# A new order for the beginning of a Fourier mixer with a low-rank channel product

## The chip, the cores and the metric

The kernel runs on one core of a Trainium2 chip. The metric is the device time of one execution in microseconds (us); lower is better. The engines are TensorE (PE, with its weight loads shown as PEld), VectorE (DVE), ScalarE (ACT), GpSimd (POOL) and the DMA queues, which SyncE (SP) and POOL issue to. Each engine works off its own list of instructions in order; semaphores hold an instruction until what it needs is there.

## The reference

```python
X = np.fft.fft(x, axis=1)              # x: 8 batches, 3136 rows, 256 channels, f32
X = np.fft.fft(X, axis=2).real         # the mixed rows
h = X.transpose(0, 2, 1) @ U @ V       # U: 3136 x 32, V: 32 x 3136, along the rows
u = X + h.transpose(0, 2, 1)
out = u + np.maximum(u @ w_ch1, 0) @ w_ch2     # 256 -> 1024 -> 256
```

## The kernel before

**Fourier transform.** The transform of a batch is two products with cosines and sines: along the 3136 rows (`seq`) and along the 256 channels (`chan`). Symmetry makes the first small. `x` is loaded as forward rows `xf` (gathers that POOL issues, one of each quarter q) and as rows read in reverse `xr` (plain DMAs from SP). VectorE folds them: `along_d` adds or subtracts channel d and 256-d (lines L350 and L352, even or odd quarters, `EV` and `OD`), into `EOF_` and `EOR_`; `alone` copies the two channels that have no partner (L356, POOL); `mirror` (L360, L363) combines forward and reverse; `half` (L368) gives `GO` (odd output rows) and `GE`, and `fourth` (L372) gives `GC` (even output rows). `seq(b, par, typ, pn)` then multiplies the folded rows with tables: `par` 1 for odd and 0 for even outputs, `typ` 0 for the sine channels and 1 for the cosine ones, and `pn` 0 and 1 for two products whose sum and difference are two mirrored halves of the output. The first product is copied out of PSUM by ScalarE (`ev`, L432); the second is joined with it by VectorE (L452 the sum into one half, L454 or L456 the difference into the other) into the rows `A` and `B`. `chan` (L473, L475) multiplies `A` and `B` with the channel tables `MC` and `MSN`, in four parts of 392 columns, and ScalarE copies the result to `S` and `T`. For sine, odd outputs, one row of `B` is negated by POOL (L465).

**Tables.** The cosine and sine tables (`TABE`, `TABO`, `TABS`) are made on the chip at the start: POOL's iota, two VectorE instructions per phase, ScalarE's sine; ScalarE copies mirrored parts, VectorE halves the entries that would count twice (`halve`, L310 and L312) and multiplies others with alternating signs (`other_even`, L344, `other_odd`, L335, with the row `srow` of -1 and 1).

**U.** The low-rank factor U goes through the same transform: `fold_u` folds it on VectorE (L209 to L223), `transform_u(t)` gives three steps: two of small matmuls (L256) and the copy of their result into spare columns of the tables. Every `seq` then yields the product with the transformed U in 32 more columns; the joins write it to `tab` (L459, L462). `lowrank` (L485, L488) turns `tab` into `TA`, and writes one row of `VA` (L489), in which V lies.

**Main loop.** The rows of all batches are taken in 49 chunks of 512. `front(c)` adds the low-rank part (L511) to `S` and `T` on VectorE (`u`, L519); `first_product` (L531) and a ReLU on ScalarE (L533) give `h`, and `second_product` (L547), added to the transposed `u` on VectorE (L553 to L556), gives the output. The fold, `seq` and `chan` of the next batches are spread between, as steps with a due number (eight per chunk).

**What sets the order.** Up to the main loop the order of each engine's instructions is that of the code (`manual_schedule`). In the main loop a planner orders them by its own reckoning of when each can start, so VectorE may do folds of a later batch ahead of a sum that stands earlier in the code. Tiles wait for their last readers; `xf`, `xr`, `EOF_`, `EOR_` and `GE` exist once, `GO`, `GC`, `VA` and `TA` twice. PSUM has three buffers of the name `dft`, three `p1` and two `p2`.

The first batch before the change: all of the U work comes ahead of the folds; the folds first make channels 0 to 127 and 256 (sine), then 128 to 255 (cosine); and then each `seq` is followed by its joins, all eight `chan`, `lowrank`, and `front(0)`.

Of the kernel before, what the change touches and what calls it, by code (L numbers as in the profile page):

```python
# [16 lines left out]
P = 128  # L17
PQ = 98
KP = PQ + 1
NI = 4  # L20
# [11 lines left out]
def kernel(  # L32
# [82 lines left out]
    nc.gpsimd.iota(xidx[:], pattern=[[S // 4, B], [S // 16, 4]], base=97, channel_multiplier=-1)  # L115
    load_0(moe_U, UF, UR, 0, R)
    load_r(moe_U, UR, 0, 0, 4, R)
    for q in range(4):
        load_f(moe_U, UF, 0, q, R)
    load_0(x, xf, xr, 0, D)  # L120
    for q0 in (1, 0):
        load_r(x, xr, 0, q0, 2, D)
    iota(kev[:, 0:NT], [[-2, 2], [-4, NT // 2]], 392)
    iota(kev[:, NT:2 * NT], [[-2, NT]], 391)
    for q in (0, 2, 1, 3):
        load_f(x, xf, 0, q, D)
# [23 lines left out]
    zeros(nc.vector, 0)  # L150

# [13 lines left out]
    srow = cpool.tile([KP, 2 * NT], BF16, name="srow")  # L165
# [31 lines left out]
    phe = gen.tile([KP, 2, 2 * NT], I32, name="phe", bufs=1)  # L197
    uy = cpool.tile([KP, 2, 2, 2, NI * R], FP32, name="uy")
# [7 lines left out]
    def fold_u():  # L206
# [12 lines left out]
        for c in range(2):  # L219
            nc.vector.tensor_tensor(GUC[c].rearrange("p t i r -> p t (i r)"), ueven[:, :, 0],  # L220
                                    ueven[:, :, 1], op=AL.add if c == 0 else AL.subtract)
            nc.vector.tensor_single_scalar(NUC[c][:], GUC[c][:, :, 2, :], -1.0, op=AL.mult)
            nc.vector.tensor_single_scalar(NUO[:, :, c, :], GUO[:, :, c, 2 - 2 * c, :], -1.0, op=AL.mult)  # L223
# [27 lines left out]
    def transform_u(t):  # L251
# [22 lines left out]
        def even_k():  # L274
            pu = PU[t] = psum.tile([P, 16, R], FP32, tag="dft", name="pu", bufs=3)
            for c, i in enumerate((3, 1)):
                for io in range(NI):
                    dst = pu[:kp(io), 2 * io + c, :]
                    if io % 2 == 0:
                        group(dst, [(wo(t, i, io, nm), go(i, nm)) for nm in range(2)])  # L280
                    else:
                        group(dst, [(we(t, i, io), gc(i, io))])
# [25 lines left out]
    def halve(t):  # L308
        for lo, hi in ((0, TE - NT), (T2, WE)):
            nc.vector.tensor_single_scalar(TABE[t][:, 3, lo:hi], TABE[t][:, 3, lo:hi], hv[:KP], op=AL.mult)  # L310
        v = TABS[t][:, 0, 1, off_t(t, 3):off_t(t, 3) + NT]
        nc.vector.tensor_single_scalar(v, v, hv[:KP], op=AL.mult)  # L312
# [12 lines left out]
    def cosine_odd(i):  # L325

        sgn = 1.0 if i == 0 else -1.0
        nc.scalar.activation(both(1, i, 1, 0, 1, NT), both(0, i, NT - 1, NT - 1, -1, NT),
                             AF.Copy, scale=sgn)
        nc.scalar.activation(TABO[1][:, 0, i // 2, 0:2 * NT], TABO[0][:, 0, i // 2, 2 * NT - 1::-1][:, 0:2 * NT],  # L330
                             AF.Copy, scale=sgn)

    def other_odd(t):

        nc.vector.tensor_tensor(TABO[t][:, 1, :, 0:2 * NT], TABO[1 - t][:, 0, :, 0:2 * NT],  # L335
                                strip(srow[:], 0, [[0, 2], [1, 2 * NT]]), op=AL.mult)

    def other_even(t):

        def cells(u, nm):  # L340
            v = TABS[u][:, nm, 0, :]
            return bass.AP(v.tensor, v.offset + off_t(u, 1),
                           [v.ap[0], [WS + off_t(u, 3) - off_t(u, 1), 2], [1, NT]])
        nc.vector.tensor_tensor(cells(t, 1), cells(1 - t, 0),  # L344
                                strip(srow[:], 0, [[0, 2], [1, NT]]), op=AL.mult)
# [8 lines left out]
    def alone(qs, src, dst):  # L354

        nc.gpsimd.tensor_copy(dst[:, qs, :, 128:257:128], src[:, qs, :, 0:129:128])  # L356
# [36 lines left out]
    def seq(b, par, typ, pn):  # L393
# [8 lines left out]
        d = ST[b]  # L402
        pt = psum.tile([P, QW], FP32, tag="dft", name="pt", bufs=3)
        mm = []

        def add(t, col, odd):

            if par == 0:
                for c in range(2):
                    g = GC[b % 2][0 if (c == 0) == (t == 1) else 1]  # L410
                    lo, hi, at = ((0, TE - NT + NE, 0), (TE - NT + NE, WE, TE - NT))[c]
                    for i in ((0, 2) if odd else (1, 3)):
                        mm.append((at, g[:kp(i), i, col:col + P], TABE[t][:kp(i), i, lo:hi]))
            else:
                for i in ((0, 2) if odd else (1, 3)):
                    at = 0 if odd else NT * slot(t, i)
                    tab = TABO[t] if odd else TABS[t]
                    for nm in range(2):
                        mm.append((at, GO[b % 2][:kp(i), nm, i, col:col + P],
                                   tab[:kp(i), nm, i // 2, :]))  # L420
        if typ == 1:
            add(1, 128, pn == 1)
        else:
            add(0, 0, pn == 1)
            add(1, 256, (pn == 1) == (par == 1))
        for n, (at, w, rhs) in enumerate(mm):
            nc.tensor.matmul(pt[:, at:at + rhs.shape[-1]], w, rhs, start=(n == 0),  # L427
                             stop=(n == len(mm) - 1), skip_group_check=True)
        if pn == 0:
            ev = d["ev"] = wp.tile([P, QW], FP32, tag="ev", name="ev", bufs=2)  # L430
            w = WO if par else QW
            nc.scalar.copy(ev[:, :w], pt[:, :w])  # L432
            if par == 1:
                eh = d["eh"] = wp.tile([P, 2 * NT], FP32, tag="eh", name="eh", bufs=2)
                nc.vector.tensor_tensor(eh[:, 0:NT], ev[:, NT - 1::-1], ev[:, WO - 1:WS - 1:-1],
                                        op=AL.subtract)
                nc.vector.tensor_tensor(eh[:, NT:2 * NT], ev[:, 0:NT], ev[:, WS:WO], op=AL.add)
            return
        ev = d["ev"]
        dst = d["A"] if typ == 1 else d["B"]  # L440
        if par == 0:
            def src(v):
                return strip(v[:], 1, [[WS, 2], [1, NT]])
# [3 lines left out]
            u0 = TE - NT  # L447
        else:
            p_, e_ = pt[:, 0:2 * NT], d["eh"][:]
            up, dn = dst[:, 783::-2], dst[:, 785:HALF:2]  # L450
            u0 = None
        nc.vector.tensor_tensor(up, p_, e_, op=AL.add)  # L452
# [4 lines left out]
        if par == 0:  # L457
            nc.vector.tensor_tensor(dst[:, 784:785], pt[:, 0:1], ev[:, 0:1], op=AL.add)
            nc.vector.tensor_tensor(d["tab"][:, typ, par, :], pt[:, TE - NT:TE - NT + NE],  # L459
                                    ev[:, TE - NT:TE - NT + NE], op=AL.add)  # L460
        else:
            nc.vector.tensor_tensor(d["tab"][:, typ, par, :], pt[:, 2 * NT:WO],  # L462
                                    ev[:, NT:WS], op=AL.add)
            if typ == 0:
                nc.gpsimd.tensor_single_scalar(dst[0:1, 785:HALF:2], dst[0:1, 785:HALF:2], -1.0,  # L465
                                               op=AL.mult)

    def chan(b, ch, h):
# [3 lines left out]
        pt = psum.tile([P, TE], FP32, tag="dft", name="pst", bufs=3)  # L472
# [6 lines left out]
    def lowrank(b):  # L479
        d = ST[b]  # L480
        pt = psum.tile([R, 256], FP32, tag="dft", name="ptt", bufs=3)
        n = 0
        for typ in range(2):
            for par in range(2):
                nc.tensor.matmul(pt[:], d["tab"][:, typ, par, :], MDT[typ][:],  # L485
                                 start=(n == 0), stop=(n == 3))
                n += 1
        nc.scalar.copy(TA[b % 2][:R, :], pt[:])  # L488
        nc.vector.tensor_tensor(VA[b % 2][R:R + 1, HALF + 1:S], d["S"][0:1, HALF - 1:0:-1],  # L489
# [76 lines left out]
    def transform(b):  # L566

        yield from fold(b)
        for par, typ in ([(1, 0), (0, 0), (1, 1), (0, 1)] if b == 0 else
                         [(0, 1), (0, 0), (1, 1), (1, 0)]):  # L570
            for pn in range(2):
                yield lambda par=par, typ=typ, pn=pn: seq(b, par, typ, pn)
# [3 lines left out]
        yield lambda: lowrank(b)  # L576
# [7 lines left out]
    nc.vector.memset(srow[:, 0:2 * NT:2], -1.0)  # L584
    nc.vector.memset(srow[:, 1:2 * NT:2], 1.0)
# [35 lines left out]
    for t in range(2):  # L621
        halve(t)
    other_even(0)
    other_even(1)
    us, uc = transform_u(0), transform_u(1)
    fold_u()
    other_odd(0)
    other_odd(1)
    us[0]()
    us[1]()  # L630
    uc[0]()
    uc[1]()
    us[2]()
    uc[2]()
    along_d(OD, xr, EOR_, 0)
    alone(OD, xr, EOR_)
    zeros(nc.gpsimd, 1)
    for s in range(2):
        nc.gpsimd.memset(VA[s][:].bitcast(I32), 0)
        nc.gpsimd.memset(TA[s][:], 0.0)  # L640
        nc.gpsimd.memset(TA[s][R:R + 1, 0:1], 1.0)
        nc.gpsimd.memset(TA[s][R:R + 1, P:P + 1], -1.0)
    nc.gpsimd.iota(pint[:], pattern=[[0, 1]], base=D, channel_multiplier=-1)
    nc.gpsimd.memset(pint[0:1], P)
    along_d(EV, xr, EOR_, 0)
    alone(EV, xr, EOR_)
    along_d(EV, xf, EOF_, 0)
    alone(EV, xf, EOF_)
    mirror(0, slice(0, 128), AL.subtract)
    mirror(0, slice(256, 258), AL.add)  # L650
# [3 lines left out]
    phase(pd[:], lrow.rearrange("p a l -> p (a l)"), pcol[:], 17)  # L654
    sine(MSN[:, 0:128], pd[:, 0:128], 17, -1)
# [4 lines left out]
    along_d(OD, xf, EOF_, 0)  # L660
    alone(OD, xf, EOF_)
    mirror(1, slice(0, 128), AL.subtract)
    mirror(1, slice(256, 258), AL.add)
# [87 lines left out]
```

## Time and profile before

| what | value |
|---|---|
| median of 3 runs | 490.22 us (490.13 to 490.26) |
| the profiled execution, its time | 490.67 us |
| the profiled execution, its span | 488.9 us |
| busy: PE, DVE, ACT, POOL | 449.7, 342.7, 273.3, 88.1 us |
| main loop, L531 and L547 together | 2352 matmuls, 413.8 us busy |
| granted TensorE clock, mean | 0.99 |

The span is what the profile's times count from. Busy times of matmuls overlap in TensorE's pipeline, so 449.7 us does not mean that many microseconds at its peak. In the lines shown below, a row of a timeline has the start, the busy time, the engine, the line of the code, the operation, what it writes and reads with the shape, and in brackets how long the engine was idle before and what ended it. A row of the chain of waits has the start, the time that the chain spends there, and the engine and line; L12 is line 12 of the kernel.

### The profile page before, as it was taken

What the parts mean: (1) busy time and instruction counts of PE and PEld (TensorE: products, weight loads), DVE (VectorE), ACT (ScalarE), POOL (GpSimd) and SP (SyncE); (2) the same over time, 40 slices, a digit from 0 to 9 for tenths busy, and PEclk for the clock granted to TensorE, in tenths of its full rate; (3) what the DMA queues carried; (4) which work ended last, traced back from release to release, by engine and by line L of the source; (5) the groups of instructions that cost most, each with busy time, mean ns of one, the idle gap of its engine ahead of it and who ended that gap; (6) DMA issues with size and microseconds to landing.
All of it is one profiled execution on the core that took longest, in us unless ns stands there. A gap on an engine that the chain in (4) does not pass through costs nothing.

```text
span 488.9 us, 8177 instructions
## 1 busy us (share of the span) xinstructions
PE 449.7 (92%) x3096; PEld 299.9 (61%) x3096; DVE 342.7 (70%) x771; ACT 273.3 (56%) x533; POOL 88.1 (18%) x109
## 2 busy tenths in 40 slices
PE   0364799999999999999999999999999999999997
PEld 0342267666766666666766676666766676666665
DVE  5999699999999999997984358343743374434333
ACT  5331655665557554765566655756466556656562
POOL 7745230424144321610010001000010001000000
PEclk9997899999999999999999999999999999999999
DMA  5778389499839995595232422334223352333433
GB/s 149 157 135 236 64 152 254 134 253 260 231 89 220 245 249 163 134 272 142 70 104 65 131 67 68 102 89 129 67 66 86 108 88 86 88 98 99 128 90 126
DMA packets 87275, 67.14 MB, mean 137 GB/s; under 512 B 53920, under 2 KB 80556, under 8 KB 87236
## 3 DMA queue, kind: packets, MB, share of 16 engines
q1 hardware_dynamic: 81588, 51.86, 41.2%
q0 software_dynamic: 5648, 14.76, 11.8%
q8 instruction: 24, 0.39, 0.3%
q14 instruction: 15, 0.12, 0.1%
HBM read 29.26 MB, written 25.69 MB: 112 GB/s over the span
## 4 chain that ended last, share of the span: by engine, by line
PE 79%; DVE 16%; issue 2%; POOL 1%; ACT 1%; DVEq 0%; POOLq 0%
PE p L547 32%; PE p L531 31%; PE pt L427 6%; PE ph L511 4%; PE pst L473 3%; PE pst L475 2%; DVE eof L352 1%; DVE B L452 1%; DVE eof L350 1%; DVE u L519 1%; DVE eor L350 1%; DVE eor L352 1%; DVE A L452 1%; DVE B L456 1%; POOL uf L56 1%
## 5 line engine op out<-in xcount | busy, mean ns | idle before, releaser
L533 ACT ACTIVATE h<-p 128x512 bf16<-128x512 f32 x392 | 218.5, 597 | 139.6 <-PE p L531 139.4
L531 PE MATMUL p<-u,w 128*128 128x512 bf16 x784 | 210.1, 379 | 2.7 <-DVE u L519 2.7
L547 PE MATMUL p<-w,h 128*128 128x256 bf16 x1568 | 203.7, 273 | 0.0
L547 PEld LDWEIGHTS <-h 128*128 128x128 bf16 x1568 | 153.1, 98 | 59.2 <-DVE o L556 0.3
L531 PEld LDWEIGHTS <-w 128*128 128x128 bf16 x784 | 75.5, 98 | 59.8 <-issue 3.8
L553 DVE TENSOR_TENSOR o<-p,ut 128x4 f32<-128x4 f32 (+1 forms) x100 | 16.1, 161 | 111.3 <-PE p L547 111.2
L56 POOL DMA_INDIRECT xf<-in_x_dram,xidx x32 | 40.2, 1257 | 72.8 <-DVE eof L352 51.4
L465 POOL TENSOR_SCALAR B<-B 1x392 bf16<-1x392 bf16 x8 | 14.6, 1823 | 181.9 <-DVE tab L462 129.7
L556 DVE TENSOR_TENSOR o<-p,ut 128x254 f32<-128x254 f32 (+1 forms) x100 | 40.5, 405 | 0.0
L555 DVE TENSOR_TENSOR o<-p,ut 128x254 f32<-128x254 f32 (+1 forms) x100 | 40.5, 405 | 0.0
L519 DVE TENSOR_TENSOR u<-ph,S 128x512 bf16<-128x512 f32 (+15 forms) x64 | 34.9, 554 | 0.1
L432 ACT COPY ev<-pt 128x424 f32<-128x424 f32 (+1 forms) x32 | 16.4, 513 | 32.9 <-PE pt L427 21.4
L519 DVE TENSOR_TENSOR u<-ph,T 128x512 bf16<-128x512 f32 (+15 forms) x64 | 34.8, 553 | 0.0
L427 PEld LDWEIGHTS <-go 98*128 98x128 bf16 x192 | 19.4, 102 | 18.9 <-DVE go L368 7.1
L511 PE MATMUL ph<-va,ta 128*128 128x512 bf16 (+18 forms) x128 | 29.7, 329 | 0.5 <-ACT ta L488 0.5
L427 PE MATMUL pt<-te,gc 98*128 98x229 bf16 (+1 forms) x192 | 24.8, 268 | 0.3 <-DVE tab L459 0.2
L473 PE MATMUL pst<-A,mc 128*128 128x392 bf16 (+1 forms) x64 | 22.7, 355 | 2.3 <-DVE A L452 1.4
L427 PE MATMUL pt<-to,go 98*128 98x424 bf16 x96 | 21.8, 367 | 2.6 <-DVE tab L462 2.6
L475 PE MATMUL pst<-B,msn 128*128 128x392 bf16 (+1 forms) x64 | 22.7, 354 | 0.0
L427 PEld LDWEIGHTS <-gc 98*128 98x128 bf16 x192 | 18.6, 100 | 6.4 <-DVE tab L459 2.8
L477 ACT CAST S<-pst 128x392 bf16<-128x392 f32 (+1 forms) x32 | 15.7, 489 | 12.1 <-PE pst L475 12.1
L256 PE MATMUL pu<-guo,ts 99*98 99x32 bf16 (+1 forms) x16 | 2.3, 239 | 19.3 <-DVE guo L213 19.3
(120 smaller groups left out, 364.1 us busy)
## 6 DMA issues: line engine op xcount, KB each, us to landing
out_dram<-o SPq DMA_DIRECT2D x48, 512.0 KB
xr<-in_x_dram SPq DMA_DIRECT2D x7, 1568.0 KB
xr<-in_x_dram SPq DMA_DIRECT2D x2, 784.0 KB
ut<-u SPq DMA_TRANSPOSE x49
xf<-in_x_dram,xidx POOLq DMA_INDIRECT x32, 6.6
w<-in_moe_w_ch_dram POOLq DMA_DIRECT2D x1, 512.0 KB, 7.8
out_dram<-o SPq DMA_DIRECT2D x4, 128.0 KB
va<-in_moe_V_dram POOLq DMA_DIRECT2D x2, 196.0 KB, 5.2
```

The lines of the kernel that those rows point to most:

```text
L56: nc.gpsimd.indirect_dma_start(out_, None, bass.AP(t.tensor, t.offset, [[w, rows], [1, w]]), bass.IndirectOffsetOnAxis(idx, 0), element_of ...
L427: nc.tensor.matmul(pt[:, at:at + rhs.shape[-1]], w, rhs, start=(n == 0), stop=(n == len(mm) - 1), skip_group_check=True)
L432: nc.scalar.copy(ev[:, :w], pt[:, :w])
L473: nc.tensor.matmul(pt[:, :hi - lo], MC[:, h * P:(h + 1) * P], d["A"][:, lo:hi], start=True, stop=False)
L475: nc.tensor.matmul(pt[:, :hi - lo], MSN[:, h * P:(h + 1) * P], d["B"][:, lo:hi], start=False, stop=True)
L511: nc.tensor.matmul(ph[:, col:col + hi - lo], TA[b % 2][:, s * P:(s + 1) * P], VA[b % 2][:, lo:hi], start=True, stop=True)
L519: nc.vector.tensor_tensor(u[:, s, col:col + hi - lo], ph[:, col:col + hi - lo], src, op=AL.add)
L531: nc.tensor.matmul(p1[:], W1[:, s, j * P:(j + 1) * P], k["u"][:, s, :], start=(s == 0), stop=(s == 1))
L533: nc.scalar.activation(k["h"][:, j, :], p1[:], AF.Relu)
L547: nc.tensor.matmul(p2[:, t % w, :], h[:, j, rs], W2[:, j, :], start=(j == 0), stop=(j == JT - 1))
L555: nc.vector.tensor_tensor(o[:, ts, 1:P], p2[:, :w, 1:P], ut[:, ts, 1:P], op=AL.add)
L556: nc.vector.tensor_tensor(o[:, ts, P + 1:D], p2[:, :w, P + 1:D], ut[:, tT, P - 1:0:-1], op=AL.add)
```

## The change

Only the beginning changes, and the first batch. In words:

- **Loads.** On SP, U's reverse rows are loaded first and x's odd reverse quarters come ahead of x's single rows. On POOL the iota `kev` stands after two of U's four gathers instead of after all four.
- **Tables.** `halve` goes from VectorE to POOL. `other_even` becomes four strided POOL instructions, `other_odd` four strided ScalarE copies; `srow` is gone. The zero columns of `GO` and `GC` of the first buffer are set by POOL.
- **Folds.** VectorE's order is: odd reverse rows, `fold_u`, even reverse rows, channel tables, forward rows. The negations of the folded U and the first batch's `alone` are ScalarE's.
- **U in the first batch.** The products of batch 0 leave out the 32 columns for U (`ne` is 0); `u_alone` computes them by 48 matmuls of its own. `transform_u(1)` stands between the products, its result in `p2`.
- **Joins.** The joins of batch 0 are split: first the outputs up to 784 (`high=False`) of all four groups, then `u_alone`, `lowrank` and the first `chan`, then the mirrored outputs (`low=False`), each followed by one `chan`. `EB` is 4, so four `ev` are kept.
- **Into the main loop.** Four `chan` steps (columns from 785) and the one-row `VA` (`mirror_row`) get the due numbers 0, 1, 4, 5 and 6.
- **The rest.** `VA` is zeroed by two memsets over partitions 32 to 63 and 64 to 127 instead of one over all. POOL's DMAs of W1, V and W2 follow the table work; the small `gate` read ahead of the second batch's loads is gone.

The diff, cut to its core:

```diff
+    load_r(moe_U, UR, 0, 0, 4, R)
     load_0(moe_U, UF, UR, 0, R)
-    load_r(moe_U, UR, 0, 0, 4, R)
-    for q in range(4):
+    load_r(x, xr, 0, 1, 2, D)
+    load_0(x, xf, xr, 0, D)
+    load_r(x, xr, 0, 0, 2, D)
+    for q in range(2):
         load_f(moe_U, UF, 0, q, R)
...
     iota(kev[:, NT:2 * NT], [[-2, NT]], 391)
+    for q in range(2, 4):
+        load_f(moe_U, UF, 0, q, R)
...
     def halve(t):
         for lo, hi in ((0, TE - NT), (T2, WE)):
-            nc.vector.tensor_single_scalar(TABE[t][:, 3, lo:hi], TABE[t][:, 3, lo:hi], hv[:KP], op=AL.mult)
+            nc.gpsimd.tensor_single_scalar(TABE[t][:, 3, lo:hi], TABE[t][:, 3, lo:hi], hv[:KP], op=AL.mult)
...
     def other_odd(t):
+        for n, sgn in enumerate((-1.0, 1.0)):
+            nc.scalar.activation(TABO[t][:, 1, :, n:2 * NT:2], TABO[1 - t][:, 0, :, n:2 * NT:2],
+                                 AF.Copy, scale=sgn)
     def other_even(t):
...
+        for n, sgn in enumerate((-1.0, 1.0)):
+            nc.gpsimd.tensor_single_scalar(cells(t, 1, n), cells(1 - t, 0, n), sgn, op=AL.mult)
...
+    def u_alone(b, tag):
+        d = state(b)
+        pt = psum.tile([P, 2, R], FP32, tag=tag, name="ptu", bufs=BUFS[tag])
+        for typ in range(2):
+            mm = []
+            for t, col in ((1, P),) if typ else ((0, 0), (1, 256)):
+                for c in range(2):
+                    g = GC[b % 2][0 if (c == 0) == (t == 1) else 1]
+                    lo = TE - NT + NE * c
+                    mm += [(g[:kp(i), i, col:col + P], TABE[t][:kp(i), i, lo:lo + NE]) for i in range(NI)]
+                for i in range(NI):
+                    tab, lo = (TABS[t], off_u(t, i)) if i % 2 else (TABO[t], 2 * NT)
+                    mm += [(GO[b % 2][:kp(i), nm, i, col:col + P], tab[:kp(i), nm, i // 2, lo:lo + NE])
+                           for nm in range(2)]
+            for n, (w, rhs) in enumerate(mm):
+                nc.tensor.matmul(pt[:, typ, :], w, rhs, start=(n == 0), stop=(n == len(mm) - 1))
+        nc.scalar.copy(d["tab"][:, :, 0, :], pt[:])
...
     for t in range(2):
+        other_odd(t)
+    for t in range(2):
         halve(t)
+    for t in range(2):
+        other_even(t)
+    zeros(nc.gpsimd, 0)
+    for part in range(2):
+        along_d(OD, xr, EOR_, part)
     fold_u()
+    negatives()
+    for part in range(2):
+        along_d(EV, xr, EOR_, part)
...
     phase(pd[:], lrow.rearrange("p a l -> p (a l)"), pcol[:], 17)
+    alone(OD, xr, EOR_, nc.scalar.copy)
+    alone(EV, xr, EOR_, nc.scalar.copy)
+    alone(EV, xf, EOF_, nc.scalar.copy)
+    alone(OD, xf, EOF_, nc.scalar.copy)
...
+    us[0]()
+    us[1]()
+    us[2]()
     nc.gpsimd.dma_start(out=W1[:, 0, :], in_=moe_w_ch1[0:P, :])
     gather(w1t[:], moe_w_ch1, D, pint[:], H, 0)
     for s in range(2):
+        nc.gpsimd.memset(VA[s][R:2 * R].bitcast(I32), 0)
+        nc.gpsimd.memset(VA[s][2 * R:P].bitcast(I32), 0)
...
+    zeros(nc.gpsimd, 1)
+    for part in range(2):
+        along_d(EV, xf, EOF_, part)
+    mirror(0, slice(0, 128), AL.subtract)
+    mirror(0, slice(128, 258), AL.add)
+    along_d(OD, xf, EOF_, 0)
+    mirror(1, slice(0, 128), AL.subtract)
+    mirror(1, slice(256, 258), AL.add)
+    for cols in (slice(0, 128), slice(256, 258)):
+        half(0, 1, cols)
+    seq(0, 1, 0, 0, "dft", False)
+    seq(0, 1, 0, 1, "p1")
+    sin_odd = dict(ST[0])
+    for cols in (slice(0, 128), slice(256, 258)):
+        half(0, 0, cols)
+        for c in range(2):
+            fourth(0, c, cols)
+    uc[0]()
+    uc[1]()
+    uc[2]()
+    seq(0, 0, 0, 0, "dft")
+    seq(0, 0, 0, 1, "p1")
+    sin_even = dict(ST[0])
+    along_d(OD, xf, EOF_, 1)
+    mirror(1, slice(128, 256), AL.add)
+    half(0, 1, slice(128, 256))
+    seq(0, 1, 1, 0, "dft", False)
+    seq(0, 1, 1, 1, "p1")
+    cos_odd = dict(ST[0])
+    half(0, 0, slice(128, 256))
+    for c in range(2):
+        fourth(0, c, slice(128, 256))
+    seq(0, 0, 1, 0, "dft")
+    seq(0, 0, 1, 1, "p2")
+    cos_even = dict(ST[0])
+    groups = ((1, 0, sin_odd), (0, 0, sin_even), (1, 1, cos_odd), (0, 1, cos_even))
+    for par, typ, kept in groups:
+        apart(0, par, kept)
+        join(0, par, typ, kept, high=False)
+    u_alone(0, "p2")
+    lowrank(0)
+    chan(0, 0, 0, "dft")
+    for par, typ, kept in groups[:3]:
+        join(0, par, typ, kept, low=False)
+        chan(*((0, 0, 1, "p1"), (0, 1, 0, "p1"), (0, 1, 1, "p1"))[groups.index((par, typ, kept))])
+    join(0, 0, 1, cos_even, low=False)
     load_x(1)
...
-    due = {}
+    due = {0: [lambda: chan(0, 2, 0)], 1: [lambda: chan(0, 2, 1)], 4: [lambda: chan(0, 3, 0)],
+           5: [lambda: chan(0, 3, 1)], 6: [lambda: mirror_row(0)]}
```

## The prediction

> **What bounds the kernel now.** I read the page first, then the beginning in the chain of waits, the timeline of POOL and PE there, and busy time by stretch. The stretches (PE, PEld, DVE, ACT, POOL, granted clock, DMA):
>
> ```profile
> 54.00:62.00 8.00, 5.68 (x26) 2.26 (x25) 7.97 (x11) 4.59 (x9) 2.13 (x2) 1.00 0.39 86
> 62.00:70.00 8.00, 7.61 (x55) 5.06 (x53) 8.00 (x13) 3.88 (x8) 4.16 (x3) 1.00 0.65 129
> 90.00:110.00 20.00, 20.00 (x139) 13.09 (x137) 19.92 (x37) 13.60 (x28) 5.22 (x4) 1.00 0.71 196
> 200.00:300.00 100.00, 100.00 (x703) 67.87 (x702) 72.36 (x161) 60.40 (x116) 7.43 (x9) 1.00 0.45 122
> ```
>
> From 62 us on TensorE is full; the loop costs what it costs, so the change is worth the time by which the loop starts earlier, less what it adds or stalls there. The loop starts with the second L531 at 55.42. What stands ahead of it is, in the chain:
>
> ```profile
> 12.40 3.85 DVE te L310 x2
> ...
> 28.70 1.80 DVE eos L363 x2
> 30.51 0.73 DVE go L368 x2
> ...
> 40.10 0.76 DVE gc L372 x2
> ...
> 47.20 0.49 PE pst L473
> ...
> 53.08 0.93 DVE va L489
> ```
>
> VectorE carries it to 47.2 (folds, then joins), then 16 matmuls of `chan` (to 52.6, about 0.33 each), the one-row `va` (0.93), and the sums `u`. Two DVE steps are too long: two halvings of 0.30 each took 3.85, the 0.69 mirror 1.72. POOL shows why:
>
> ```profile
> 13.50 0.54 POOL L146 MEMSET go<- 99x504 int32 x1
> 14.46 1.42 POOL L639 MEMSET va<- 128x1568 int32 x1
> 28.85 1.03 POOL L689 CAST w<-w1t 128x1024 bf16<-128x1024 f32 x1
> 144.07 3.55 POOL L465 TENSOR_SCALAR B<-B 1x392 bf16<-1x392 bf16 x1
> ```
>
> The halving stood still until POOL's unbroken run of memsets ended at 16.13; the mirror grew by 1.03, the length of the CAST. At 144.07 the reverse: a 1.30 us POOL step takes 3.55 while two DVE folds (1.20, 1.21, no longer than elsewhere) run.
>
> TensorE in the first batch:
>
> ```profile
> 31.21 1.70 PE L427 MATMUL pt<-ts,go 98*128 98x228 bf16 x8 [4.37 <-DVE go L368]
> 32.70 2.86 PE L427 MATMUL pt<-to,go 98*128 98x424 bf16 x8
> 35.40 1.75 PE L427 MATMUL pt<-te,gc 98*128 98x229 bf16 x16
> ```
>
> The first 16 run at half pace (0.35 for 424 columns), the next at 0.109 each. I call the first of these starts T0: 31.2 now. T0 to loop start is 24.2.
>
> **What the change does to T0.** DVE drops 0.97 us of zero memsets and 0.44 of `srow`; `kev` comes after two U gathers instead of four (2 x 1.27 earlier). ACT's table work (8.75 to 15.65, 6.9 long) then starts near 6.2 and ends at 13.1; the four alternating-sign copies it takes over (rows like L330, 0.42 apart) end at 14.8. It is not last. The x rows issued first on SP let DVE do both odd reverse folds (2 x 1.13) before U is there, so they are free. The U fold waits for its last gather: in before issued at 6.28, landed 7.9 later; now pushed back 0.6 by `kev`: 14.8. Behind that, to T0, DVE has: U fold 3.5 (17.09 to 21.18 less four negations, now ACT), even reverse 2.27, phase of the channel tables 0.9, even forward 2.27, mirrors 1.4, odd forward half 1.13, mirror 0.78, odd half 0.75: 13.0. T0 would be 27.8. x lands at 18.7 to 21.8 in the trace (gathers issued at 8.05 to 11.99, 9.8 to 11.0 to land; their issue times stay), before each fold needs it. `us` on TensorE (about 3.2, as `uc`) needs the strips: with POOL done by 24 it ends at 27.2, before T0; each microsecond that POOL is later than 28 would move T0. The four `alone` pairs go to ACT (0.25 each on POOL), idle there; without that cover they would cost 1.0.
>
> Against it: POOL takes over six halvings and four sign strips, each 196 columns, from 13.7 on (after gathers to 12.94 and small iotas). No row has 99x196 on POOL. The 1x392 TENSOR_SCALAR gives 0.65 each by halves; the 1024-column CAST at 1.03 against the 16-column one at 0.25 gives 0.39. So 3.9 to 6.5 us, of which 2.8 to 5.4 lie after 14.8, where DVE wants two SBUF inputs. By the CAST row the one waits for the other, and POOL holds first. I take 4.1, the middle, since the operation is L465's but the layout of six is the CAST's. T0 = 31.9, no earlier than now. If POOL waits instead, DVE loses nothing (27.8).
>
> The Trainium skill, page "SBUF — State Buffer", section "Who interferes with whom", says that a DVE instruction with two SBUF inputs contends with a GpSimd instruction that reads SBUF, not with one that only writes. The trace agrees on both: 1.72 beside the CAST, but L209 its usual 0.42 beside the second VA memset (16.38 to 17.79). By that rule alone the whole 2.8 to 5.4 stands and the zero memsets moved to POOL are free; the page "GPSIMD Engine Reference", section "Engine selection", calls one-input work there roughly line-rate, by which the lower end would hold and the time be 1.3 us less than my sum.
>
> **From T0 to the loop.** Now TensorE is the longer chain, because DVE's remaining folds (5.4) and lower joins (0.95 to 1.0 per group, last one when its product is done) end at T0+12. TensorE: 8 products of 196 columns at the slow pace 1.46, 8 of 392 columns 2.64; `uc`, moved in here, 36 matmuls, 3.2 (23.66 to 26.84); 16 sin-even at 0.109, 1.75; cos-odd 1.1; cos-even 0.87: T0+11.0. Then `u_alone`, new: 2 x 16 + 16 = 48 matmuls. The nearest rows are `uc`'s 0.088 and L427's 0.109 and, slow, 0.2125: 4.2, 5.2 or 10.2; I take 4.2, as these have uc's 32 columns and follow 15 us of work. Copy 0.36, low rank 0.3, first `chan` pair 0.33, four ACT copies of 0.49: T0+18.2; sums: loop at T0+19.0, 5.2 shorter than 24.2. Most is four `chan` pairs instead of eight slow ones, upper joins beside TensorE, and `va` out of the way.
>
> Loop start: 31.9 + 19.0 = 50.9 against 55.4: -4.5.
>
> **What comes late next.** Four `chan` pairs (1.33) move into the loop. They fill a hole: TensorE waits 1.25 at 60.53 for the second chunk's `u`. Cover gone, they cost 1.3. `va` (0.93, DVE) is due at step 6, needed at the fourth chunk: free unless DVE stalls.
>
> POOL's queue is the other worry. Behind the strips come zeros (1.0), W1's DMA and gather (3.3), VA and TA twice (7.6, since two partition ranges make two memsets of 1.35), CAST and W2 (2.5), zeros (1.0): from 24 to 39. V lands by 43, W2 (7.8) by 48, before use; VA's memset to V's DMA has 8 us of slack. Then the sign row of B waits for the first upper join (T0+12.5) and runs 1.3, and behind it in the queue are the next batch's x gathers: issued T0+13.8 to T0+17.6, the third, which the even fold needs, at T0+16.3. With 6.1 to land (the loop's rows show 4.2 to 7.7) it is there at T0+22.4. Now it lands 4 us before DVE asks; after, DVE is free at T0+19.1. SP's reverse rows, no longer behind the `gate` read, are there early, so DVE can do two reverse folds (2.27) first: stall 1.0, which TensorE feels through `u` of chunk 1, queued behind.
>
> Sum: -4.5 + 1.0 = -3.5. The profiled run took 490.67 for a span of 488.9 (1.8 around it), 0.45 above the median of the runs, 490.22. Span 485.4, median 486.7.
>
> **Rivals.**
> 1. Next x late: DVE's order has the even forward fold ahead, as at 55.29 now. Stall 22.4 - 19.1 = 3.3: -1.2, so 489.0. For: today's order. Against: that order was made where x had landed.
> 2. Slower: the same order with 10.7 us from issue to landing, as the gathers of 35.9 to 42.5 had. Third gather at T0+27.0, stall 7.9: +3.4, 493.6. It decides from 7.3 us on (stall over 4.5). Against: those shared the DMA engines (0.95 to 1.05 busy) with the reverse rows, which now come earlier.
> 3. POOL yields to DVE, as at 144.07: T0 27.8, time 482.6. For: that row. Against: POOL is there first, and folds that depend on one another leave it openings (the 0.25 CAST at 98.86 got in after 1.10).
> 4. It doesn't do what it says: `u_alone` at the slow pace for half or all of it gives back 3.0 or 6.0: 489.7 to 492.7; strips starved past T0 would do the same. Against: TensorE is without a pause from T0.
>
> **Numbers.** Forecast (-2 to -6) 0.42; rival 1 0.20, of which 0.07 falls within 0.2% (1 us, about what can be told from no change); rival 2 0.16; rival 3 0.12; rival 4 0.10, half within. Faster 0.42 + 0.13 + 0.12 = 0.67; same 0.07 + 0.05 = 0.12; slower 0.16 + 0.05 = 0.21. The range reaches from just below rival 3 (482) to the middle of rival 4's upper half (491.5); rival 2 and the rest of rival 4, some 0.18, are left out.
>
> **What would show it.** Right: U fold starting near 14.8, its steps or the even reverse fold drawn out by 3 to 5 us beside POOL TENSOR_SCALARs; first L427 near 32; 48 matmuls of about 0.09; loop near 51; a DVE wait on `xf` of about 1 us behind the first `u`. Wrong: first L427 near 28, or x landing over 7.3 us after the gathers with TensorE waiting for `u` of the second chunk.

## The result: slower by half a per cent

The changed kernel takes 492.48 us (median of 20 runs, 490.04 to 494.25), the kernel before 489.75 (20 runs, 489.09 to 490.74): ratio 1.005, with an interval of 1.0038 to 1.0062. Forecast were 486.7 us (482.0 to 491.5) and faster. The profiled execution of after has a span of 490.6 (before 488.9) and took 492.45. Lines have moved: L427 is L431 now, L519 is L569 (`u`), L531 and L547 are L581 and L597, the folds L350 and L352 are L355 and L357, the sign row L465 is L492.

**The beginning is shorter, by far more than forecast.** TensorE's timeline of after (start, busy time, engine, line, operation, idle time before):

```profile
28.60 1.49 PE L431 MATMUL pt<-ts,go 98*128 98x196 bf16 x8
29.88 2.82 PE L431 MATMUL pt<-to,go 98*128 98x392 bf16 x8
...
40.52 0.36 PE L511 MATMUL ptu<-te,gc 98*128 98x32 bf16 x8
...
46.38 0.38 PE L581 MATMUL p<-u,w 128*128 128x512 bf16 x1 [0.22 <-DVE u L569]
...
60.06 2.03 PE L581 MATMUL p<-u,w 128*128 128x512 bf16 x4 [8.44 <-DVE u L569]
61.89 1.81 PE L597 MATMUL p<-w,h 128*128 128x256 bf16 x8
```

T0 is 28.60 (31.21 before, 31.9 forecast). The second L581, which starts the loop, is at 46.38 (55.42 before, 50.9 forecast): 9.0 us earlier. But the second chunk's first product is at 60.06, after a pause of 8.44; before, it was at 60.53 after 1.25. All of the 9.0 us but 0.5 is gone there.

**Who makes the pause.** VectorE's timeline of after:

```profile
45.64 0.68 DVE L569 TENSOR_TENSOR u<-ph,T 128x512 bf16<-128x512 f32 x1
46.24 1.21 DVE L355 TENSOR_TENSOR eor<-xr 99x1016 bf16<-99x1016 f32 x1
54.77 1.22 DVE L355 TENSOR_TENSOR eof<-xf 99x1016 bf16<-99x1016 f32 x1 [7.32 <-issue]
55.91 1.22 DVE L357 TENSOR_TENSOR eof<-xf 99x1016 bf16<-99x1016 f32 x1
57.05 1.22 DVE L355 TENSOR_TENSOR eor<-xr 99x1016 bf16<-99x1016 f32 x1
58.19 1.22 DVE L357 TENSOR_TENSOR eor<-xr 99x1016 bf16<-99x1016 f32 x1
59.33 0.68 DVE L569 TENSOR_TENSOR u<-ph,S 128x512 bf16<-128x512 f32 x1
```

After the first chunk's `u` VectorE does one reverse fold, stands for 7.32, and then does four folds of the second batch ahead of the second chunk's `u`. Before, there were four folds and no wait; so the second `u` gains 9.0 by the start, loses 7.3 by the wait and 1.1 by the fifth fold, and comes at 59.33 instead of 59.79. VectorE stands for the forward rows, which POOL asks for:

```profile
42.66 1.32 POOL L492 TENSOR_SCALAR B<-B 1x392 bf16<-1x392 bf16 x1 [0.93 <-DVE B L486]
44.15 1.05 POOL L56 DMA_INDIRECT xf<-in_x_dram,xidx  x1 [0.17 <-issue]
45.50 1.00 POOL L56 DMA_INDIRECT xf<-in_x_dram,xidx  x1 [0.30 <-issue]
46.80 1.49 POOL L56 DMA_INDIRECT xf<-in_x_dram,xidx  x1 [0.30 <-issue]
48.59 0.96 POOL L56 DMA_INDIRECT xf<-in_x_dram,xidx  x1 [0.31 <-issue]
```

The gathers stand in POOL's queue behind the sign row, which waits for a join. Before they were issued from 35.9 on, 19.5 us ahead of the loop; now 2.2 us ahead. The third, which the even fold needs, lands 7.9 after its issue, at 54.7. The chain of waits of after has the pause as `issue` (the wait itself has no record) and the same folds behind it:

```profile
48.36 6.41 issue
54.77 0.17 DVE eof L355
...
59.40 0.61 DVE u L569
...
60.06 2.03 PE p L581 x4
```

By stretch (length, then PE, PEld, DVE, ACT, POOL, granted clock, DMA share, GB/s), after:

```profile
54.00:62.00 8.00, 1.94 (x5) 0.64 (x6) 7.20 (x8) 0.60 (x1) 6.26 (x5) 0.67 0.14 46
62.00:70.00 8.00, 8.00 (x53) 5.32 (x52) 7.97 (x13) 3.85 (x7) 2.16 (x2) 0.91 1.19 102
90.00:110.00 20.00, 20.00 (x138) 13.03 (x137) 19.95 (x38) 13.74 (x28) 7.03 (x8) 1.00 0.86 217
200.00:300.00 100.00, 100.00 (x703) 67.87 (x702) 68.69 (x157) 60.32 (x116) 4.97 (x5) 1.00 0.42 109
```

From 54 to 62 TensorE works 1.94 us (5.68 before). From 62 to 70 and from 90 to 110 it is full again; over the whole of 62 to 200 it stands for 2.7 us, before for 1.6. VectorE is full from 60 to 110 in both kernels (7.97 of 8 in the second row, 19.95 of 20 in the third), so what it lost by standing it cannot win back soon. The clock column adds something: granted was 0.50 from about 57 to 63, and the first products behind the pause take 2.03 and 1.81 where later groups of the same size take 1.03 and 1.04.

**Where the difference stands, chunk by chunk.** The transposed read of each chunk's `u` is issued (L572) when that `u` is done. Its time after, less that of before: chunk 0 -9.12, chunk 1 -0.47, chunk 3 -0.18, chunk 8 +1.13, chunk 16 +2.03, and +1.73 from chunk 22 to the end, which is the difference of the spans. So 8.65 us go between chunks 0 and 1, and 2.2 more up to chunk 22. The experiments use this ledger. Each ledger is that of one profiled execution, while the 20 runs of the changed kernel lie within 4.2 us, so differences of a few tenths between two ledgers say little.

### The profile page after: what moved, and what is told of

Its sections match the earlier page's. It is cut to its first block, busy times and chain, and to the rows that moved or that the text cites. A ratio compares the mean times of both kernels' runs of the same rounds, so it can differ in the third digit from the quotient of the medians.

```text
span 490.6 us, 8293 instructions
## 1 busy us (share of the span) xinstructions
PE 449.1 (92%) x3142; PEld 301.2 (61%) x3142; DVE 333.9 (68%) x747; ACT 277.0 (56%) x546; POOL 104.2 (21%) x120
## 4 chain that ended last, share of the span: by engine, by line
PE 62%; DVE 22%; issue 5%; DMA 1%; DVEq 0%; ACT 0%
PE p L597 26%; PE p L581 25%; PE pt L431 5%; DVE u L569 3%; PE ph L561 3%; DVE eor L355 2%; DVE eor L357 2%; DVE o L606 2%; DVE eof L355 2%; PE pst L522 1%; PE pst L524 1%; DVE eof L357 1%; DVE o L605 1%; DVE ge L373 1%; DVE B L478 1%
## 5 line engine op out<-in xcount | busy, mean ns | idle before, releaser
L581 PE MATMUL p<-u,w 128*128 128x512 bf16 x784 | 211.7, 380 | 9.4 <-DVE u L569 9.4
L597 PE MATMUL p<-w,h 128*128 128x256 bf16 x1568 | 204.5, 273 | 0.0
L597 PEld LDWEIGHTS <-h 128*128 128x128 bf16 x1568 | 153.4, 98 | 60.0 <-issue 0.6
L581 PEld LDWEIGHTS <-w 128*128 128x128 bf16 x784 | 75.7, 98 | 65.6 <-DVE u L569 8.9
L492 POOL TENSOR_SCALAR B<-B 1x392 bf16<-1x392 bf16 x8 | 11.3, 1412 | 193.3 <-DVE tab L489 104.7
L56 POOL DMA_INDIRECT xf<-in_x_dram,xidx x32 | 35.3, 1103 | 52.5 <-DVE eof L357 40.8
L569 DVE TENSOR_TENSOR u<-ph,S 128x512 bf16<-128x512 f32 (+15 forms) x64 | 35.0, 555 | 0.1
L569 DVE TENSOR_TENSOR u<-ph,T 128x512 bf16<-128x512 f32 (+15 forms) x64 | 34.9, 555 | 0.0
L447 ACT COPY ev<-pt 128x425 f32<-128x425 f32 (+3 forms) x32 | 16.3, 510 | 23.9 <-PE pt L431 21.8
L431 PE MATMUL pt<-te,gc 98*128 98x229 bf16 (+2 forms) x192 | 25.0, 271 | 1.8 <-DVE tab L489 1.8
L261 PE MATMUL pu<-guo,ts 99*98 99x32 bf16 (+1 forms) x16 | 2.4, 245 | 25.1 <-POOL ts L317 18.2
L431 PEld LDWEIGHTS <-go 98*128 98x128 bf16 x192 | 19.8, 103 | 8.9 <-issue 1.4
L355 DVE TENSOR_TENSOR eof<-xf 99x1016 bf16<-99x1016 f32 x16 | 19.5, 1216 | 7.3 <-issue 7.3
L361 POOL CAST eof<-xf 99x16 bf16<-99x16 f32 x14 | 15.3, 1094 | 42.8 <-DVE eos L368 17.4
L431 PEld LDWEIGHTS <-gc 98*128 98x128 bf16 x192 | 18.9, 102 | 7.4 <-DVE tab L489 4.3
L522 PE MATMUL pst<-A,mc 128*128 128x392 bf16 (+1 forms) x64 | 21.2, 331 | 1.2 <-DVE tab L489 0.9
L355 DVE TENSOR_TENSOR eor<-xr 99x1016 bf16<-99x1016 f32 x16 | 19.3, 1209 | 3.4 <-DMA xr<-in_x_dram 3.4
```

Of the source, the lines that this page charges most:

```text
L56: nc.gpsimd.indirect_dma_start(out_, None, bass.AP(t.tensor, t.offset, [[w, rows], [1, w]]), bass.IndirectOffsetOnAxis(idx, 0), element_of ...
L355: nc.vector.tensor_tensor(dst[:, qs, :, 1:128], lo, hi, op=AL.subtract)
L522: nc.tensor.matmul(pt[:, :hi - lo], MC[:, h * P:(h + 1) * P], d["A"][:, lo:hi], start=True, stop=False)
L569: nc.vector.tensor_tensor(u[:, s, col:col + hi - lo], ph[:, col:col + hi - lo], src, op=AL.add)
L581: nc.tensor.matmul(p1[:], W1[:, s, j * P:(j + 1) * P], k["u"][:, s, :], start=(s == 0), stop=(s == 1))
L597: nc.tensor.matmul(p2[:, t % w, :], h[:, j, rs], W2[:, j, :], start=(j == 0), stop=(j == JT - 1))
```

## Experiments

Theory A: the late rows of the second batch hold VectorE, and all that is queued behind their folds. Theory B: the rows may be late; what costs is that the second chunk's `u` is ordered behind the folds. Theory C: whatever the start wins, the loop's new work takes back. Times and ratios are against the kernel before on the same chip; each edit is made on the changed kernel unless said. "Ends" are the last values of the ledger.

**1. The gathers early (e1_x_early).** All loads of the second batch right behind the first batch's last read of `xf`, the work on W2 behind these loads, and the second `VA` with its zeros behind the joins:

```diff
-    for s in range(2):
+    def v_part(s):
...
+    v_part(0)
...
+    load_x(1)
     (msr, W1, W2)
...
-    load_x(1)
+    zeros(nc.gpsimd, 1)
+    v_part(1)
```

> The changed kernel, with the second batch's x gathers issued on POOL right behind the first V (as soon as the odd forward fold has read xf, about 34 to 38 us instead of 44 to 49), and the second VA, the second zero columns moved behind the first batch's joins. Theory A (VectorE stands still from 47.5 to 54.8 because the third gather, issued at 46.8, lands at 54.7, and all that stands behind it in VectorE's order is late by that): the gather lands near 45, the hole of 8.4 us on TensorE goes, the loop starts near 46.4 as before and the time falls by 7 to 9 us against the changed kernel, to about 484. Theory B (only the place of the second chunk's sum behind the folds counts): the folds are still ahead of the sum, so at most the wait for x goes and 4.5 us of folds stay: 3 to 4 us less. Theory C (VectorE's and TensorE's order in the loop takes back what the beginning gains, wherever it starts): no more than 1 us less.

Measured: 483.0 us (before 489.54), ratio 0.9851 (0.9813 to 0.9888), 9.5 under the changed kernel's 492.48. The gathers go at 34.46 to 38.44 and land after 5.0 to 6.3 us. VectorE's timeline of this run has no pause left:

```profile
46.35 0.68 DVE L569 TENSOR_TENSOR u<-ph,T 128x512 bf16<-128x512 f32 x1
46.95 1.21 DVE L355 TENSOR_TENSOR eof<-xf 99x1016 bf16<-99x1016 f32 x1
...
52.08 0.68 DVE L569 TENSOR_TENSOR u<-ph,S 128x512 bf16<-128x512 f32 x1
```

The same four folds still stand ahead of the second `u` (one mirror as well); it comes at 52.08 instead of 59.33. Ledger: -8.41, -7.72, -7.22 in the first three chunks, and it ends at -6.65. A stands. C is out as the main cause: the start's gain is mostly kept when the rows are there.

**2. The gathers a little earlier, a little later (e2_x_before_sign, e3_x_later).** Ahead of the sign row; and behind two further memsets of `VA`:

```diff
     chan(0, 0, 0, "dft")
+    load_x(1)
     for par, typ, kept in groups[:3]:
...
     join(0, 0, 1, cos_even, low=False)
-    load_x(1)
```

```diff
     join(0, 0, 1, cos_even, low=False)
+    for _ in range(2):
+        nc.gpsimd.memset(VA[1][2 * R:P].bitcast(I32), 0)
     load_x(1)
```

(the first as e2, ahead of the join with the sign row in it; the second as e3, ahead of the gathers.)

> The changed kernel, with the second batch's loads ahead of the upper joins, so that POOL issues the gathers before it waits for the sign row of B: 41.7 instead of 44.15, 2.4 us earlier, and nothing else. Theory A: third gather lands near 52.3, time 2.4 us less (490). Theory B: as A, 2 us. Theory C: no change.

> The changed kernel, with two more memsets of 1.41 us on POOL ahead of the second batch's gathers: 2.8 us later. Theory A: time 2.8 us more (495.3). Theory B: the same. Theory C: no change, since the loop would absorb it.

Measured: 492.06 (1.0052, 1.0023 to 1.0081) and 492.42 (1.0062, 1.0043 to 1.0082): neither moved, so the numbers that A gave for these small shifts missed. The third gather landed at 53.7 and 56.0, after 8.1 and 5.5 us. But the planner changed the order with it. Between the landing and the second `u` the changed kernel has four folds; e2, with its rows 1.0 earlier, has four folds and a mirror (0.6), and e3, with its rows 1.3 later, two folds and a mirror, the other two folds ahead of the wait. So the second `u` comes at 58.95 and 58.99, against 59.33. What counts is the landing plus the folds that are ordered behind it, and the two moved against each other. The ledgers of e2 and e3 stand at -0.85 and -0.81 at chunk 1, below the changed kernel's -0.47, and still end above it, at +2.01 and +1.81: behind the pause they lose more, by a slow clock that lasts longer (priced under "Why the prediction was wrong").

**3. The other order of VectorE (e4_u1_first, e5_both).** The first four products of chunk 0, two `chan` and `front(1)` ahead of the planned part, so that the second `u` precedes the folds; e5 is this with the early loads of e1:

```diff
+    for j in range(4):
+        first_product(0, j)
+        if j < 2:
+            chan(0, 2, j)
+    front(1)
```

> The changed kernel, with the first four first products, the two chan of the third part and the second chunk's sums written out by hand ahead of the planned loop, so that VectorE does the second chunk's sums before any fold of the second batch. x comes as late as before (54.7). Theory A: the second chunk starts near 51.5, but the folds still start at 54.8, and the third chunk's sums stand behind 12 us of them: TensorE waits there instead (from about 58 to 68) and the time falls by no more than 1.5 us. Theory B: the wait was that of the second chunk alone: 6 to 8 us less.

> The early gathers of e1_x_early together with the hand-written start of e4_u1_first (second chunk's sums ahead of all folds). Theory A: with x there in time the order counts: the second chunk's sums come near 50 instead of 52.1, TensorE's 3.4 us of waits in e1 shrink to about 1.5, and the time falls to about 481.5 (1 to 2 us under e1). Rival: VectorE, full from 47 to 115 in either order, hands the delay to the third chunk: same as e1, 483.

Measured: e4 493.0 (1.0063, 1.0044 to 1.0082). The second `u` is done early, at 50.11, yet VectorE stands 4.29 for the rows at 55.69, the third chunk's `u` is at 69.02, and TensorE now waits 7.7 in all for the outputs `o`. The pause has moved one chunk on. B falls. e5: 486.65 (0.9937, 0.9916 to 0.9958), so worse than e1 alone: chunk 1 stands at -9.86 (e1 -7.72), but chunk 2 at -4.23 (e1 -7.22) and the end at -4.06; TensorE waits 3.3 for `o`. With VectorE full, a sum done earlier is a fold done later.

**4. The rows' own order (e11_q_order).** The four gathers of the second batch in the order 0, 2, 1, 3, so that the two that the even fold needs are first:

```diff
-        for q in range(4):
+        for q in ((0, 2, 1, 3) if b == 1 else range(4)):
```

> The changed kernel with the second batch's gathers in the order 0, 2, 1, 3, so that the two that the first fold needs are issued first (44.2 and 45.5 instead of 44.2 and 46.8). VectorE's order puts the forward fold right behind the first chunk's sums, as in e2_x_before_sign, where the second chunk's sums came 4.5 to 5.2 us behind the landing. Theory A (that fold waits for its two gathers, and the time follows the second chunk's sums): landing near 51.5 to 52, the second chunk's sums at 56.5 to 57.5 instead of 59.3, time 2 us less than the changed kernel, about 490.3. Rival (the loop takes it back, as with e2): 492.

Measured: 489.77 (1.0002, 0.9984 to 1.0019), 2.7 under the changed kernel. VectorE's timeline:

```profile
51.09 1.22 DVE L355 TENSOR_TENSOR eof<-xf 99x1016 bf16<-99x1016 f32 x1 [6.35 <-issue]
...
56.26 0.68 DVE L569 TENSOR_TENSOR u<-ph,S 128x512 bf16<-128x512 f32 x1
```

The forward fold starts at 51.09 instead of 54.77, the second `u` at 56.26 instead of 59.33; the ledger ends at -1.24, 3.0 below the changed kernel's. The loop started 1.6 earlier as well (-10.71 at chunk 0), which the pause hides. This is the small shift of A that experiment 2 missed, and it agrees: 3 us of the second `u`, 3 us of the end.

**5. What else the loop loses (e6_before_join_order, e7_filler).** e6 is the kernel before with the changed join's first column and four `ev` buffers:

```diff
-            ev = d["ev"] = wp.tile([P, QW], FP32, tag="ev", name="ev", bufs=2)
+            ev = d["ev"] = wp.tile([P, QW], FP32, tag="ev", name="ev", bufs=4)
...
+        if par == 0:
+            nc.vector.tensor_tensor(dst[:, 784:785], pt[:, 0:1], ev[:, 0:1], op=AL.add)
...
-            nc.vector.tensor_tensor(dst[:, 784:785], pt[:, 0:1], ev[:, 0:1], op=AL.add)
```

> The kernel before, with only the part of the change that reaches the later batches: in the joins the single column 784 ahead of the mirrored half, and four ev buffers instead of two. Between the third and the last chunk, the changed kernel and its variants lose 0.55 us (e1 to e4) on the kernel before, besides what follows a hole. Theory: the joins' order does it: +0.5 us over the kernel before, visible between the third chunk and chunk 22 of the profile. Rival: it comes from the beginning (where the planned loop starts): no change.

Measured: 489.33 (0.9986, 0.9976 to 0.9996); ledger -0.89 at chunk 0, -1.16 at the end. Those edits in the joins are not the loop's loss.

e7 puts 32 products whose result nobody reads into the pause, to keep TensorE at work:

```diff
+            if c == 1 and j == 0:
+                p0 = psum.tile([P, CH], FP32, tag="p2", name="p0", bufs=2)
+                for n in range(32):
+                    nc.tensor.matmul(p0[:], W1[:, 0, 0:P], CK[0]["u"][:, 0, :], ...)
```

> The changed kernel with 32 idle matmuls of 512 columns (6.9 us, result unused) between the first chunk's first products and the second's, so that TensorE is busy in its hole of 8.4 us. Theory: about 1 us of the loss is TensorE's half pace after the hole (granted clock 0.5 from 57 to 61.5): with the filler it starts the second chunk at full pace, and the time falls by 0.7 to 1.3 us to about 491.4. Rival: VectorE sets the pace after the hole anyway: no change (492.5), or more if the filler outlasts the hole.

Measured: 503.12 (1.0285, 1.0248 to 1.0321). Inconclusive: the planner ordered more folds ahead of the third `u`, TensorE waited 6.0 us for `u` between 44 and 110, and the ledger ends at +8.68. And the clock was not kept up: after a pause of only 1.6, up to 60.54, the granted clock was 0.60 from 61 to 62 and 0.50 from 62 to 64.

**6. POOL's strips (e8_strips_dve, e9_strips_alone).** e8 gives the ten strips (four sign strips, shown here, and six halvings) to VectorE; e9, one profiled execution, does four strips once more (they compute what is there already) behind the gathers, while VectorE stands:

```diff
-            nc.gpsimd.tensor_single_scalar(cells(t, 1, n), cells(1 - t, 0, n), sgn, op=AL.mult)
+            nc.vector.tensor_single_scalar(cells(t, 1, n), cells(1 - t, 0, n), sgn, op=AL.mult)
```

```diff
     load_x(1)
+    for t in range(2):
+        other_even(t)
```

> The changed kernel with the six halvings and the four sign strips on VectorE instead of POOL, the rest as it is. In the prediction POOL's strips were to hold VectorE up by 4.1 us; the profile shows T0 at 28.6, with POOL's strips drawn out to 12.5 us instead. Theory (POOL is the one that waits, VectorE loses under 1 us to it): VectorE does the strips while it waits for x and U, T0 moves by less than 1 us, POOL's later work starts 10 us earlier, and since the gathers still wait for the sign row of B the time is the same within 1 us. Rival (VectorE loses some 3 us to the strips): T0 near 26 to 27 and the whole beginning earlier by 2 us or more.

> The changed kernel with the four sign strips made a second time on POOL, with the same values, behind the second batch's gathers, where VectorE stands still (47.5 to 54.8). It gives the price of one strip with nothing beside it. The prediction's bounds were 0.39 and 0.65; in the table work they took 0.81 to 1.34 beside VectorE's folds. If they take 0.6 to 0.7 here, the rest was waiting for VectorE; if about 0.8, POOL's own pace was misjudged by half and the waiting is the smaller part.

Measured, e8: 492.28 (1.0025, 0.9993 to 1.0057), T0 28.17, only 0.43 earlier. That is not all that VectorE had lost to POOL. VectorE's timelines of after and of e8, and POOL's CAST in e8:

```profile
25.41 1.35 DVE L355 TENSOR_TENSOR eof<-xf 99x1016 bf16<-99x1016 f32 x1
26.80 0.80 DVE L368 TENSOR_TENSOR eos<-eor,eof 99x1024 bf16<-99x1024 bf16 x2
27.85 0.78 DVE L373 TENSOR_TENSOR go<-eos 99x1024 bf16<-99x1024 bf16 x2 [0.25 <-POOL go L148]
```

```profile
24.67 1.21 DVE L355 TENSOR_TENSOR eof<-xf 99x1016 bf16<-99x1016 f32 x1
25.91 1.49 DVE L368 TENSOR_TENSOR eos<-eor,eof 99x1024 bf16<-99x1024 bf16 x2
27.42 0.78 DVE L373 TENSOR_TENSOR go<-eos 99x1024 bf16<-99x1024 bf16 x2
```

```profile
25.60 1.18 POOL L709 CAST w<-w1t 128x1024 bf16<-128x1024 f32 x1
```

The two kernels are level at 16.2 (L215). From there after falls 0.89 behind up to the mirror L368 and then waits 0.25 for POOL's zeros, so VectorE had lost about 1.1 us to POOL. In e8 the CAST, now earlier, draws out the mirror by 0.69 and hides most of the gain. POOL's timelines, of after (beside VectorE's folds), then of e9 (VectorE idle), then of e8:

```profile
18.09 3.35 POOL L315 TENSOR_SCALAR te<-te,hv 99x197 bf16<-99x197 bf16 x2
...
23.35 4.04 POOL L350 TENSOR_SCALAR ts<-ts 99x196 bf16<-99x196 bf16 x4
```

```profile
49.65 2.88 POOL L350 TENSOR_SCALAR ts<-ts 99x196 bf16<-99x196 bf16 x4
```

```profile
28.12 0.58 POOL L150 MEMSET gc<- 99x252 int32 x2
42.61 1.31 POOL L492 TENSOR_SCALAR B<-B 1x392 bf16<-1x392 bf16 x1 [13.91 <-DVE B L486]
44.10 1.07 POOL L56 DMA_INDIRECT xf<-in_x_dram,xidx  x1 [0.17 <-issue]
```

Alone a sign strip costs 0.72. Ten would be 7.2, if the halvings cost the same; in after they take 12.5 (14.83 to 27.3), so some 5.3 are waiting for VectorE. And in e8 POOL is done at 28.7 and idle for 13.91, and the gathers still go at 44.10: not POOL's load holds them, but the sign row in front of them. The second `u` of e8 is 1.46 earlier than in after (ledger -1.93 at chunk 1), yet the ledger ends at +1.41, only 0.3 below after's: as in e2 and e3, more is lost behind the pause.

**7. The best version (e10_fold_in_gap).** e1 with the strips on VectorE, the two even gathers (q 0 and 2) issued first, and the second batch's even forward fold in VectorE's wait for the first batch's products:

```diff
+    for q in (0, 2):
+        load_f(x, xf, 1, q, D)
...
+        if kept is sin_odd:
+            for part in range(2):
+                along_d(EV, xf, EOF_, part)
```

> e1_x_early with the strips on VectorE (as e8), the gathers of quarters 0 and 2 issued as soon as the first batch's even forward fold has read xf (about 24), and the second batch's even forward fold written by hand into VectorE's order behind the first low join, where VectorE stood still for 2.7 us waiting for TensorE (35.6 to 38.4). Theory A: two of the four folds ahead of the second chunk's sums are gone, so these come 2 us earlier than in e1 (50 instead of 52.1); time 1.5 to 2.5 us under e1, about 481. Rival: x lands after 35.6 or TensorE is short of joins, and e1's 483 stays or gets worse.

Measured: 481.35 us (480.94 to 481.89; before 489.98), ratio 0.9829 (0.9813 to 0.9846), 1.65 under e1. VectorE's timeline:

```profile
34.49 1.21 DVE L355 TENSOR_TENSOR eof<-xf 99x1016 bf16<-99x1016 f32 x1
35.62 2.05 DVE L357 TENSOR_TENSOR eof<-xf 99x1016 bf16<-99x1016 f32 x1
...
44.55 0.69 DVE L569 TENSOR_TENSOR u<-ph,S 128x512 bf16<-128x512 f32 x1
...
49.13 0.69 DVE L569 TENSOR_TENSOR u<-ph,S 128x512 bf16<-128x512 f32 x1
```

Two folds are done in the gap, the second `u` is at 49.13, and the ledger keeps the whole start: -9.61 at chunk 0, -9.35 at the end.

## Why the prediction was wrong

- **T0, the term of the strips.** Forecast 27.8 + 4.1 = 31.9, measured 28.60. The first part held within 0.8. Of the 4.1, VectorE lost about 1.1, of which 0.25 was a wait for POOL's zeros, for which the sum has no term. For the rest POOL waited for VectorE, not VectorE for POOL, so rival 3 came nearest on T0. The page "SBUF — State Buffer" of the Trainium skill, section "Who interferes with whom", says that a VectorE instruction with two SBUF inputs contends with a GpSimd instruction that reads SBUF. The trace agrees, and it shows who paid: 5.3 us on POOL, 1.1 on VectorE (three of its folds took 1.35 instead of 1.20). The price of one strip was mis-sized too: 0.39 to 0.65 forecast, 0.72 alone.
- **T0 to the loop.** Forecast 19.0, measured 17.8. The term mis-sized is `u_alone`: 48 matmuls at 0.088 make 4.2, measured 1.4 (40.52 to 41.9, about 0.025 each up to the last start). The rest held in order (`uc` before the second half of the products, four `chan` pairs ahead of the loop, `va` out of the way), but not to the tenth: the products ended at T0+11.9 instead of T0+11.0, and from `u_alone`'s end to the loop it took 4.5 instead of 3.8. Rival 4 did not occur.
- **What comes late next.** This is the step that failed the forecast. It named the mechanism (gathers behind the sign row, rows that land after VectorE asks) and priced it at 1.0; VectorE stood 7.32. By its own terms: the third gather was put at T0+16.3 and went at T0+18.2 (1.9); its landing at 6.1 and took 7.9 (1.8); VectorE was put free at T0+19.1 and was free at T0+17.6, because `u_alone` was short (1.5); and two reverse folds were put ahead of the wait where one was (1.1). With the 1.0 forecast that makes 7.3. So what the start won behind T0 only made the wait longer, since the gathers hang on a join. Rival 2 had this mechanism, with a stall of 7.9 and "decides from 7.3 us on"; its place was right, its landing of 10.7 was too long.
- **The sum.** A pause was priced as its own length. Not in it are the fifth fold (1.1) and 2.2 us more between chunk 1 and chunk 22. The slow clock is most of the 2.2. In the table its price is TensorE's busy time behind the pause, times what the granted clock lacks of 1.00, summed over quarter microseconds; beside it stands what the ledger loses from chunk 1 to the end. All six runs have the long pause of TensorE before the second chunk:

| run | after | e11 | e3 | e9 | e2 | e8 |
|---|---|---|---|---|---|---|
| lost from chunk 1 to the end, us | 2.2 | 2.3 | 2.6 | 2.7 | 2.9 | 3.3 |
| price of the slow clock, us | 1.7 | 2.1 | 2.4 | 2.5 | 2.6 | 2.9 |

  The clock leaves 0.2 to 0.5 in each. The two with 0.5 left, after and e8, are also the two in which TensorE waits 2.7 us for joins from 62 us on; the other four wait 1.5, as before does with its waits for joins and `u` together. This is a comparison of runs: no edit changed the clock alone (e7 was to do that and did not). And a kernel without a pause loses something too, with the clock at 1.00 throughout: from chunk 1 on e10 loses 0.3 and e1 1.1, which is not explained here.
- **Right:** the tables on ScalarE (their last copies end at 15.7, 14.8 forecast) and x's odd folds ahead of U are off the path. From 200 us on TensorE is full as before.

The range missed because every rival changed one term of the forecast. What happened is rival 3's start with rival 2's stall, together: 482.6 + 6.9 (7.9 for the 1.0 in the sum) = 489.5, and the fifth fold and the 2.2 make 492.8, against 492.48 measured. This sum was made after the result.

## What to carry to other kernels

When a start is shortened, ask of each load that the next stage needs what its issue hangs on: a load queued behind a step of the old critical path keeps its distance to that path, and the gain turns into a wait for it. Price the wait as landing time plus all work that is ordered behind the landing on the waiting engine, and look whether that engine is full afterwards, since then nothing is won back. Add the slow clock of TensorE behind a long pause: here it cost 1.7 to 2.9 us. The cure here was not the order on the waiting engine (e4, e5) but the place of the load in its queue (e1), and then work of the next stage in the gaps of the start (e10).

## What the hardware showed that was not expected

- Matmuls of 32 columns cost 0.083 apart in `uc` (32.49 to 35.5, 98 or 99 weight columns) and about 0.025 in `u_alone` (128 weight columns). In `uc` the weights from `to` and `ts` are read with a step and those from `te` without one; both are 0.083 apart (35.17, 35.25, 35.34 and 35.42 are starts of `te` ones), so the step does not do it. That the number of columns does was not tried.
- A sign strip on POOL took 0.72 with VectorE idle; ten strips took 1.25 on average beside VectorE's folds, which grew by 0.15 at most. At 144.07 in the profile of before it was the same. POOL's CAST of 1024 columns did the reverse in three runs: the mirrors of before and of e8 grew by 1.03 and 0.69, and the fold of e10 at 35.62 took 2.05 instead of 1.21. Why the strips wait and the CAST does not was not tried.
- The third gather landed 7.7 to 8.1 us after issues between 45.6 and 47.9 (after, e2, e4) and 5.5 after one at 50.48 (e3). A transposed read of the first chunk is under way in the former; its part was not measured, and e11's second gather, issued at 45.61 beside one, took 5.4.
- The granted clock fell 2.1 to 5.3 us after TensorE's last product (2.1 in e11, 5.0 in after, 5.3 in e2) and was back at 1.00 some 3.4 to 5.7 us after the restart (3.4 in after, 5.7 in e8). So a shorter pause is not always the cheaper one: e8's, of 7.0 us, cost 2.9 by the clock, after's, of 8.4, cost 1.7. In e7 it fell to 0.50 within 2 us of the restart after a pause of 1.6, though the 32 products had run until 58.9.
